# A two-part mLSTM and token-mixing kernel, rewritten: decays of chunk 0 from 0/1 products, values without padding, shared PSUM places, a new order of tasks

## Chip, core and metric

The kernel runs on one core of a Trainium2 chip. The metric is device time in microseconds (us) of that core for one launch; lower is better. PE is the engine for matrix products (PEld its weight loads), DVE the vector engine, ACT the scalar engine with its function tables, POOL the general engine, SP the engine that issues most DMA transfers.

## What is computed

Sizes: 4 batches, 8 heads, 768 tokens, 40 values per head; 320 channels. The first part is an mLSTM: per head a state `C` (40x40) and a vector `n` decay and grow from token to token, and are read with the query.

```python
m_new = np.maximum(f_gate[:, :, t] + m, i_gate[:, :, t])
f_stab = np.exp(f_gate[:, :, t] + m - m_new)
i_stab = np.exp(i_gate[:, :, t] - m_new)
C = f_stab[..., None, None] * C + i_stab[..., None, None] * np.einsum('bhd,bhe->bhde', vt, kt)
n = f_stab[:, :, None] * n + i_stab[:, :, None] * kt
h_tilde = np.einsum('bhde,bhe->bhd', C, qt)
denom = np.maximum(np.abs(np.einsum('bhd,bhd->bh', n, qt)[:, :, None]), 1.0)
y[:, :, t] = 1.0 / (1.0 + np.exp(-o_gate[:, :, t])) * h_tilde / denom
```

The second part takes these rows `x` (4 x 768 x 320), turns each number by an angle, mixes tokens, and ends with a channel product:

```python
theta = x @ w_theta
zr, zi = x * np.cos(theta), x * np.sin(theta)
u = x + np.einsum('ts,bsd->btd', w_tok_r, zr) + np.einsum('ts,bsd->btd', w_tok_i, zi)
return u + np.maximum(u @ w_ch, 0.0)
```

## The kernel before

The 768 tokens are cut into six chunks of 128. A **unit** is one batch in one chunk (24 units, four to a chunk), a **pair** is two batches in one chunk (12 pairs). Within a chunk the mLSTM is done as masked attention; what earlier chunks leave comes in through the state.

**Gates** (`gate_part`, `gates_rest`): scans on DVE give each head's running sums of decays; they are written to DRAM (`g_first`, `g_rest`, `e_d`) and read back by `unit_loads` as tables that are the same on all partitions (`dt`, `eb`). Only unit 0 gets its table from PE (`spread`, L741).

**A unit** (`score`, `attention`): PE forms scores `sc` (L337), upper and lower 64 rows in turn, two heads at a time. ACT takes exponentials of `dt` with a bias per head (L360), POOL masks them (L364), DVE multiplies with the scores (L370). PE multiplies these weights with the values into `ph` (L382), and q, faded on DVE or POOL (L455), with the state (L377). The values are stored with zeros between the heads, so that a product of each head writes 123 columns, the 41 of three heads. DVE or ACT, DVE, DVE form size, maximum and reciprocal of the denominator (L391, L389, L395, L396); the output gate is scaled on POOL, DVE or ACT (L404, L402) and applied on DVE (L411). Keys are faded (L417, L419), PE forms the chunk's new state `st` (L425), DVE or ACT masks it into `cn` (L436, L440), and POOL or DVE adds it to the faded state (L448, L449, or L445).

**A pair** (`mixer`, `mix_part`, `mix`): PE turns the rows over (L560) and forms angles with a three-product split of numbers into high and low parts (L597, 18 products of 320 columns; channel block 2 in 64-row halves). Angles are rounded (L605, L607, L610), sine and cosine taken on ACT, multiplied with x and split again (L633, L636, L639). Then ten groups of six products of 384 columns mix tokens (L506), each group into one of two single PSUM banks (`ps_m`, tile `pm`); DVE adds each into `acc` (L513; chunk 0 L515 to L520). Weights arrive as 64-bit numbers and are split on DVE, ACT and POOL (`split`, L249 to L271).

**The end** (`channel`, L864 to L894): `acc` is split once more into `u`, and 204 products (48 over 64 rows) form the channel product with ReLU and sum on DVE.

**What sets the order**: a table of numbers, `ORDER`, names every task with its engine letter (V DVE, A ACT, G POOL, T PE, D SP), and `Plan.issue` writes them out in that order; each engine takes its instructions strictly in it. PSUM has eight banks: `sc0`, `sc1`, `ph`, `st`, the pair `pt`, and two of `pm`.

Of the kernel before, what the change touches and what calls it, by code (L numbers as in the profile page):

```python
# [21 lines left out]
HP = 9  # L22
NR = B * HP
E1 = D + 1
VG = 7 * E1
NG = 3 * B
QR = 64 + D
NT = B * DM // P
TH = S // 2
GROUPS = tuple((c,) for c in range(NC))  # L30
# [4 lines left out]
PIECE = 512  # L35


PAR = dict(load=-8328, wload=-8347, sgload=-2808, exps=860, score=867, mult=173, pv=-1216, X=-126, st=1806, upd=-1500,
           tr=-2000, theta=-645, ang=-1907, z=-255, mix=3437, wdec=2329, sig=-5151, grest=-643, wch=22567, u0=32000,
           u1=32000, out0=18267, out1=27456, tab=3960, slack=155, zm0='V', zm1='V', zl0='G', zl1='G', wlo='G', cup='G',  # L40
           ulo='GG', ab='A', s0=-2609, s1=-11037, s2=-11454, s3=-9068, wth=-6011, w0=-734, w1=-3805, w2=-1051,
           wdup=-8318, kh='A', qh='A', kl='G', ql='V', qk=-6000, m0=7, m1=23, gst=2, slackT=67, dsg0=19, dsg1=140,
           did=61, dh0=123, dt0=115, dth=133, dh1=81, dd1=70, dt1=150, dw=145, du2=89, dmask=26, dgr=25, sg0=-1128,
           cw=17892, clr=-6830)
# [8 lines left out]
99V 52D 45A 183V 102V 109T 103V 100A 184V 262A 189V 185G 268D 186V 253G 110A 263T 46V 269D 111V 104G 53A 190T 112A
249D 54V 113A 280A 193V 101G 267D 55V 114V 271V 319D 115A 56V 254A 116V 191V 117G 192V 57G 322D 194T 48V 118A 272A
255G 256V 327A 49V 257T 195V 273G 230D 196V 119V 236D 50A 328G 270T 264A 258V 259V 260V 320A 339D 274V 51G 340D 261V
265G 133T 231A 123T 237A 323D 134A 197V 281T 232V 198A 143T 324D 233V 325T 238V 242D 275T 124A 144A 329V 199G 345A
410D 202V 343T 341D 276V 335G 128T 277V 326V 140T 203V 282A 428D 204V 129A 141V 278G 200A 411D 125T 142A 279V 283G
234A 330T 126V 127A 201V 342D 239V 416A 336T 235G 429D 331V 220T 337V 346G 223T 412D 221V 222V 243A 338G 347V 213T
240A 224A 135T 392D 434A 214V 417G 130T 136V 413D 332V 244V 414T 132A 137A 284T 131V 333G 418V 483D 120T 285A 344G
334V 138T 121V 435G 286V 122A 205T 139A 245V 287V 415G 210T 246A 398D 207V 241G 206V 288T 211V 212V 247V 393A 424G  # L60
228T 289V 353G 208T 290V 229A 399V 291A 354T 400V 292A 348T 394V 395V 432T 209A 349V 404D 350V 396A 293V 215T 296V
294A 225T 501D 216V 351G 297A 436V 217A 397G 481D 227A 218T 352V 226V 295V 405A 419T 219V 298G 430D 355V 401V 303T
420V 356G 484D 482A 357T 304V 487T 502D 358V 425T 421V 359V 402A 422G 313T 426A 431D 360V 403G 309T 423V 489A 485D
314V 427V 361T 310V 406V 486D 433G 311T 554D 362V 507A 490G 301T 363V 572D 312V 497G 437T 491V 442A 508G 302V 488V
505T 364V 555A 573D 438V 439V 365A 407V 443T 509V 440G 299T 560D 444V 576T 445V 408A 590D 317T 441V 366G 578A 300V
498T 504D 318V 492T 369V 645D 409V 370V 371V 503D 561A 305T 367V 493A 494V 368V 307T 591D 306V 495G 499V 386T 506G
496V 308V 574D 446T 387V 500G 515A 382T 447V 378T 448V 596A 579G 575D 449V 516T 379V 450T 580V 586A 597G 383V 577V
594T 451V 376T 452V 663D 380T 598V 453A 454A 510T 377V 381V 562V 563V 388T 517A 592D 511V 455G 390T 564A 389V 372T
512V 456A 646D 565V 513A 391V 458G 649T 373V 374T 734D 457V 459A 384T 514V 518G 375V 643D 651A 581T 385V 556V 593D
# [12 lines left out]
779G 710T 835V 912D 836V 780A 841V 837G 963T 711V 782G 838V 704T 960D 698T 705V 783V 843T 781V 696T 699V 784G 846V
706T 965A 697V 842V 708T 707V 913D 725V 714T 726V 878D 727V 905T 715V 709V 966G 884D 844V 845V 787T 906A 962D 907V
908V 847T 909V 961D 788V 879V 967V 797T 974D 848A 885V 964V 793T 849V 798V 977T 794V 850V 801T 915V 851A 886V 919T
802V 887V 979A 852V 795T 976D 920V 855G 789T 796V 975D 921V 785T 922V 923V 790V 888A 924T 980G 786V 856A 968T 927V
889G 925V 857V 799T 853V 969A 970V 971V 700T 800V 854G 926V 791T 701V 978G 972V 864T 792V 880V 870T 865V 928T 871V
881V 882V 890D 981V 883G 874T 929V 1024D 862T 875V 930V 982T 863V 931A 891V 932A 892V 876T 983V 984V 893V 860T 985G
877V 1030D 894A 858T 986V 895G 861V 1022V 987T 859V 866T 990V 712T 988A 867V 989V 872T 933G 713V 991T 873V 936V 934V
937A 935G 803T 992V 868T 993V 938G 804V 869V 1023A 994A 945T 1025V 1026V 995A 951T 1027V 946V 1036D 1031A 996V 939T
1028A 952V 999G 997A 957T 940V 1029V 949T 1000A 958V 998G 1037A 943T 950V 1001V 947T 944V 1032V 1046A 1014T 1033V  # L90
1034V 1015V 1035G 948V 1038V 1048A 1018T 1039V 1020T 1019V 1040A 1049V 1012T 1021V 1041V 1087A 1002T 1013V 1042G 955T
1003V 941T 956V 1047V 1052A 1004T 942V 1043G 1044A 1010T 1005V 1006T 1011V 1079V 1083A 953T 1045G 1007V 1008T 954V
1050V 1016T 1009V 1051G 1081A 1059T 1017V 1085A 1054T 1084G 1060V 1056T 1055V 1053G 1061T 1057V 1058D 1086V 1066T
1062V 1082G 1063D 1080G 1074T 1067V 1064T 1075V 1088G 1089T 1065V 1068D 1099T 1090V 1111T 1100V 1094T 1112V 1076T
1095V 1071T 1077V 1078D 1069T 1072V 1101T 1070V 1073D 1109T 1102V 1103D 1106T 1110V 1113D 1096T 1107V 1091T 1097V
1098D 1104T 1092V 1093D 1105V 1108D
""".split()


class Plan:  # L100


    def __init__(self):
        self.waiting = []

    def add(self, eng, us, prio, fn, after=(), table=None, cols=0, follow=(), bank=None, pick=None, dmas=1):
        alts = None
        if isinstance(eng, dict):
            alts, fn0 = eng, fn
            eng = pick or next(iter(alts))  # L110
            us = alts[eng]
            fn = lambda: fn0(t.eng)
# [5 lines left out]
    def clash(self, some, others):  # L118

        for a in some:  # L120
            for b in others:
                a.clash.append(b)
                b.clash.append(a)
# [14 lines left out]
def mlstm_mixer(ctx: ExitStack, tc: tile.TileContext, gates, qk, q3, tok, og,  # L138
# [662 lines left out]
    for n in range(NU):  # L801
# [9 lines left out]
        if n % 2:  # L811
            mixer(q)
# [168 lines left out]
```

## Time and profile before

| | |
|---|---|
| three timed runs | 396.33, 392.63, 395.36 us, median 395.36 |
| profiled execution | span 388.3 us; the page gives no time of its own beside it |
| busy in that span | PE 329.2 (85%), PEld 297.2, DVE 300.0 (77%), ACT 205.2 (53%), POOL 164.2 (42%) |
| DMA | 66.81 MB in 51,506 packets |
| chain that ended last | PE 34%, DVE 28%, DMA 23%, ACT 6%, issue 5% |
| first and last token-mixing product | 72.2 us, 344.2 us |

A row of the page's groups gives line, engine, operation, output<-input, shape and count, then busy us, the mean ns of one, and the idle time before it with what ended it. In the slices each digit is a fortieth of the span, in tenths of busy time.

### The profile page before, as it was taken

How to read it: one execution, taken by the hardware profiler on the slowest of the kernel's cores; microseconds unless marked ns; L12 is line 12 of the kernel's file. 1: busy time of each engine (PE TensorE's matmuls, PEld its weight loads, DVE VectorE, ACT ScalarE, POOL GpSimd, SP SyncE). 2: the span in 40 equal slices, each digit the busy share in tenths (PEclk: the TensorE clock that was granted, in tenths of full speed). 3: DMA queues.
4: the chain of work that ended last, by engine and by line, in shares of the span. 5: the costliest groups of instructions: out<-in, count | busy, mean ns of one | idle time of the engine just before them, and what ended most of it. 6: DMA issues, size and time to landing. Idle time of an engine off the chain costs nothing.

```text
span 388.3 us, 6289 instructions
## 1 busy us (share of the span) xinstructions
PE 329.2 (85%) x2231; PEld 297.2 (77%) x2231; DVE 300.0 (77%) x559; ACT 205.2 (53%) x478; POOL 164.2 (42%) x146
## 2 busy tenths in 40 slices
PE   4468743986899979889899889999989987999995
PEld 3357632885798869779789789989988976888884
DVE  4858728995688878698699989999999989854222
ACT  2675748982653964788788755843440433320000
POOL 1518233564627245265113755555133442475000
PEclk9657966999899999999999999999999999999999
DMA  6979999699517999559783794838640101302134
GB/s 169 259 275 321 251 261 265 164 265 218 163 57 219 252 232 241 134 152 292 192 263 93 237 290 147 215 92 229 190 158 13 56 1 41 69 0 83 41 122 162
DMA packets 51506, 66.81 MB, mean 172 GB/s; under 512 B 3112, under 2 KB 39436, under 8 KB 51476
## 3 DMA queue, kind: packets, MB, share of 16 engines
q1 hardware_dynamic: 50259, 65.12, 59.1%
q0 software_dynamic: 1216, 1.31, 1.8%
q8 instruction: 17, 0.28, 0.3%
q14 instruction: 14, 0.11, 0.1%
HBM read 60.97 MB, written 4.13 MB: 168 GB/s over the span
## 4 chain that ended last, share of the span: by engine, by line
PE 34%; DVE 28%; DMA 23%; ACT 6%; issue 5%; SPq 2%; POOL 1%; DVEq 0%; POOLq 0%; ACTq 0%
PE pm L506 12%; PE pm L888 10%; DMA eb<-e_d 8%; DMA q_t<-in_q 5%; DVE acc L513 5%; PE pt L597 3%; PE ph L382 3%; DMA dt<-g_rest 3%; DMA sg<-in_og 3%; ACT dt L360 2%; DVE val L257 2%; PE sc L337 2%; DVE dt L370 2%; DVE val L261 2%; DVE C L445 2%
## 5 line engine op out<-in xcount | busy, mean ns | idle before, releaser
L506 PE MATMUL pm<-w,z 128*128 128x384 f32 x480 | 96.7, 349 | 9.2 <-ACT acc L515 5.3
L506 PEld LDWEIGHTS pm<-w,z 128*128 128x128 f32 x480 | 83.4, 191 | 14.1 <-ACT acc L515 5.9
L382 PE MATMUL ph<-tok_t,dt 128*128 128x123 f32 x384 | 57.1, 287 | 5.8 <-DMA tok_t<-in_tok 4.8
L360 ACT ACTIVATE dt<-dt,bwT 128x128 f32<-128x128 f32 x184 | 56.1, 390 | 11.1 <-DMA dt<-g_rest 8.1
L513 DVE TENSOR_TENSOR acc<-pm,acc 128x384 f32<-128x384 f32 x100 | 53.6, 549 | 8.5 <-PE pm L506 8.0
L382 PEld LDWEIGHTS ph<-tok_t,dt 128*128 128x128 f32 x384 | 51.0, 201 | 7.1 <-ACT acc L582 2.9
L506 PE MATMUL pm<-wsm,z 128*128 128x384 f32 x240 | 46.6, 344 | 7.4 <-DVE acc L513 7.3
L506 PEld LDWEIGHTS pm<-wsm,z 128*128 128x128 f32 x240 | 41.0, 188 | 11.2 <-DVE acc L513 11.1
L364 POOL TENSOR_SCALAR_AFFINE_SELECT dt<-dt 128x1024 f32<-128x1024 f32 (+1 forms) x26 | 30.2, 1162 | 38.8 <-ACT dt L360 35.7
L888 PE MATMUL pm<-u,w 128*128 128x384 f32 (+1 forms) x204 | 40.2, 351 | 0.0
L597 PE MATMUL pt<-wthp,xs 128*128 128x320 f32 (+1 forms) x198 | 32.3, 339 | 7.5 <-DVE xs L576 7.5
L888 PEld LDWEIGHTS pm<-u,w 128*128 128x128 f32 (+1 forms) x204 | 33.0, 187 | 7.0 <-issue 7.0
L597 PEld LDWEIGHTS pt<-wthp,xs 128*128 128x128 f32 (+1 forms) x198 | 26.0, 196 | 12.5 <-issue 12.4
L404 POOL TENSOR_TENSOR sg<-sg,den 128x320 f32<-128x320 f32 x15 | 13.0, 867 | 46.9 <-DVE den L396 46.5
L337 PE MATMUL sc<-qk 40*128 40x128 f32 x368 | 27.6, 291 | 5.1 <-DMA qk<-in_qk 5.1
L894 DVE SCALAR_TENSOR_TENSOR acc<-pm,acc 128x384 f32<-128x384 f32 x20 | 11.1, 557 | 26.7 <-PE pm L888 26.7
L370 DVE TENSOR_TENSOR dt<-sc,dt 128x512 f32<-128x512 f32 x46 | 29.4, 678 | 2.4 <-POOL dt L364 2.4
L337 PEld LDWEIGHTS sc<-qk 40*128 40x128 f32 x368 | 23.2, 193 | 9.8 <-issue 4.5
L377 PE MATMUL ph<-C,q_t 120*128 120x123 f32 x120 | 23.7, 279 | 3.9 <-DVE X L411 2.7
L377 PEld LDWEIGHTS ph<-C,q_t 120*128 120x128 f32 x120 | 18.8, 190 | 5.3 <-issue 1.9
L417 ACT ACTIVATE tok_t<-tok_t,bwT 128x40 f32<-128x40 f32 x64 | 14.7, 314 | 10.5 <-DMA tok_t<-in_tok 10.5
L455 POOL TENSOR_TENSOR q_t<-q_t,eb 120x384 f32<-120x384 f32 x11 | 12.4, 1127 | 18.2 <-DMA eb<-e_d 18.2
(117 smaller groups left out, 552.9 us busy)
## 6 DMA issues: line engine op xcount, KB each, us to landing
tok_t<-in_tok SPq DMA_DIRECT2D x24, 610.5 KB
dt<-g_rest SPq DMA_DIRECT2D x20, 512.0 KB
qk<-in_qk SPq DMA_DIRECT2D x24, 416.0 KB
raw<-in_wtok SPq DMA_DIRECT2D x18, 512.0 KB
sg<-in_og SPq DMA_DIRECT2D x12, 320.0 KB
out<-acc SPq DMA_DIRECT2D x10, 384.0 KB
q_t<-in_q SPq DMA_DIRECT2D x20, 180.0 KB
eb<-e_d SPq DMA_DIRECT2D x60, 60.0 KB
```

The source lines that it names most:

```text
L337: nc.tensor.matmul(u.sc[s][:, hp], u.qk[rows, 1, hp], u.qk[rows, 0, hp], start=True, stop=True)
L360: nc.scalar.activation(u.dt[:, h, :], src, AF.Exp, bias=bwT[:, c, r:r + 1])
L364: nc.gpsimd.affine_select(d, d, pattern=[[0, h1 - h0], [1, P]], compare_op=ALU.is_ge, fill=0.0, base=0, channel_multiplier=-1)
L370: nc.vector.tensor_mul(d2[:, s], u.sc[s], d2[:, s])
L377: nc.tensor.matmul(u.ph[:, gg * 3 * E1:(gg + 1) * 3 * E1], u.q3[:, gg, :], C[b][:, gg, :], start=True, stop=False)
L382: nc.tensor.matmul(u.ph[:, gg * 3 * E1:(gg + 1) * 3 * E1], u.dt[:, h, :], among(h), start=(c == 0 and h == 3 * gg), stop=(h == min(3 * gg ...
L404: ENG[e].tensor_mul(u.s3, u.s3, u.den.broadcast_to([P, H, D]))
L417: nc.scalar.mul(k3[:, h], k3[:, h], bwT[:, c, 64 + HP * b + h:64 + HP * b + h + 1])
L506: nc.tensor.matmul(pm[:, :TH], x.z[:, a, s, j * P:(j + 1) * P], w[x.c][:, b, s, th * TH:(th + 1) * TH], start=(k == 0), stop=(k == last))
L513: nc.vector.tensor_add(a, pm[:, :TH], a)
L597: nc.tensor.matmul(S_.th[:, b - b0, :DM], p.xs[a0:a1, a, k, :], wt5[a0:a1, s, k, :], start=(n == 0), stop=(n == 8))
L888: nc.tensor.matmul(pm[:, :TH], E_.w[s][a0:a1, col:col + P], us[pr, k][a0:a1, a, ts], start=(n == 0), stop=(n == 3 * len(ks) - 1))
```

## The change

The whole body is rewritten. What is computed and the split into chunks, units, pairs and groups stay. By parts:

- **Chunk 0's decays**: the running sums of all heads are split into high and low parts on two halves of the partitions, and four products per unit of a 0/1 matrix with them (L278, L283) write all eight heads' exponents into two PSUM banks. ACT takes two exponentials of 512 columns per unit there (L401) in place of eight of 128 with a bias. The DRAM tables serve chunks 1 to 5 only.
- **DRAM layout**: decay tables are stored chunk by chunk, so that a unit's table is one run of 4 KB per partition (L405), q and its decays one of 1.5 KB (L393, L394; the decays in one transfer in place of three). Tokens take 688 numbers in place of 1221.
- **Values without zeros**: a head's product writes its own 41 columns (L446).
- **Output**: the maximum with 1 is taken in the gate's instruction, on DVE always (L457).
- **State**: faded in place (L488, L490) and grown straight from PSUM in three instructions per unit (L501).
- **Halves**: the 64-row products of angles and of the channel part stand in pairs, lower and upper in turn (L537, L655).
- **PSUM**: three places of two banks (`two`) for scores, chunk 0's decays, transposes, angles, mixing groups and the channel part, and two single banks (`one`) for `ph` and `st`. A mixing group is now 12 products into a two-bank place, gathered in one instruction of 768 columns (L590).
- **Weights**: split in pieces of 768 columns; copies between partition halves on ACT and DVE, where POOL issued DMAs.
- **Order**: a new table of 1009 entries.

```diff
+    two = slots("two", 3, [2, 512], pool=ps)
+    one = slots("one", 2, [512], pool=ps)
...
+    def assemble(u):
+        lw = hi_t.t.rearrange("p a s n -> p (a s n)")[:, P:2 * P]
+        gm = GMt[u.c]()
...
+        for f in range(2):
+            r = slice(64 * f, 64 * f + 64)
+            nc.tensor.matmul(u.dd.t[:, f, :], selr[r, 33 + b:34 + b].broadcast_to([64, P]), gm[r], start=False, stop=True)
...
-            src = g_d[0][rows, :] if c == 0 else g_d[1][rows, (c - 1) * P:c * P]
-            nc.sync.dma_start(u.dt, src.unsqueeze(0).broadcast_to([P, H, P]))
+            load(f"dt{n}", lambda: dma(u.E.t.rearrange("p h t -> p (h t)"), g_d[c, b * H:(b + 1) * H].rearrange(
+                "h t -> (h t)").unsqueeze(0).broadcast_to([P, H * P])), [u.E], n - 2.2)
...
-                        nc.tensor.matmul(u.ph[:, gg * 3 * E1:(gg + 1) * 3 * E1], u.dt[:, h, :], among(h),
+                    nc.tensor.matmul(u.ph.t[:, h * E1:(h + 1) * E1], u.E.t[:, RANK[h], :], v1,
...
+            nc.vector.scalar_tensor_tensor(s3(), u.den.t.broadcast_to([P, H, D]), 1.0, s3(), op0=ALU.min, op1=ALU.mult)
...
+                    nc.vector.scalar_tensor_tensor(cv[:, :k, j], st[:, :k, j], own[:KD, j:j + 1], cv[:, :k, j],
+                                                   op0=ALU.mult, op1=ALU.add)
...
+        def rest(e):
+            for l, (x, y) in enumerate(parts):
+                for b in range(2):
+                    rows = slice(64 * b, 64 * b + 64)
+                    nc.tensor.matmul(th.t[:, b, :DM], xs.t[rows, x, 2], wt5[rows, y, 2], start=False, stop=(l == 2))
...
+                for t in range(2):
+                    k = 0
+                    for s in (1, 0):
+                        for x, y in parts:
+                            nc.tensor.matmul(pm.t[:, t, :TH], z.t[:, x, s, j * P:(j + 1) * P], wv(c, y, s, t),
+                                             start=(k == 0), stop=(k == 5))
+                            k += 1
...
+                add(f"ga{q}{j}", "V", lambda e, j=j, pm=pm, av=av: nc.vector.tensor_add(av, pm.t[:, :, :TH], av), [pm],
```

Three places in the order show what moves. First SP, after its first two transfers. Before (`dt` is a decay table, `tok_t` tokens, `wsm` the gates):

```order
L296 DMA qk<-in_qk 104x1024
L173 DMA g_first<-wsm 36x128
L296 DMA qk<-in_qk 104x1024
L701 DMA sg<-in_og 128x640
L302 DMA dt<-g_first 128x1024
L306 DMA tok_t<-in_tok 128x1221
L173 DMA g_rest<-wsm 36x640
```

Of the change:

```order
L343 DMA raw_80<-in_wth 128x480
L389 DMA qk_96<-in_qk 128x1024
L389 DMA qk_97<-in_qk 128x1024
L343 DMA raw_81<-in_wth 128x480
L379 DMA sg_106<-in_og 128x640
L390 DMA tok_99<-in_tok 128x688
L379 DMA sg_107<-in_og 128x1280
```

No decay table stands among the first transfers any more; the angle weights have moved to the front, and tokens are shorter.

Second PE, where a pair's angles are formed in the middle of the kernel. Before (`pm` a mixing group, `pt` angles, `ph` output):

```order
L425 MATMUL st<-tok_t 120x123 x3
L506 MATMUL pm<-w,z 128x384 x12
L597 MATMUL pt<-wthp,xs 128x320 x18
L506 MATMUL pm<-w,z 128x384 x12
L377 MATMUL ph<-C_97,q_t 128x123
L382 MATMUL ph<-tok_t,dt 128x123 x3
```

Of the change:

```order
L446 MATMUL one_76<-tok_101,E_93 128x41 x2
L531 MATMUL two_73<-wth,xs_89 128x320 x12
L537 MATMUL two_73<-wth,xs_89 128x320 x6
L425 MATMUL two_72<-qk_98 128x128 x8
L425 MATMUL two_74<-qk_97 128x128 x8
L480 MATMUL one_76<-tok_101 120x123 x2
L480 MATMUL one_76<-tok_101 120x82
L575 MATMUL two_73<-w_899,z_77 128x384 x12
L575 MATMUL two_74<-w_899,z_77 128x384 x12
```

Angles, two units' scores and two mixing groups follow one another through the same three places, 72 to 74; the 64-row products (L537) stand by themselves.

Third DVE, around a unit's output. Before:

```order
L391 TENSOR_SCALAR den<-ph 128x8
L395 TENSOR_SCALAR den<-den 128x8
L396 RECIPROCAL den<-den 128x8
L404 TENSOR_TENSOR sg<-sg,den 128x320
L411 TENSOR_TENSOR X<-ph,sg 128x320
L436 TENSOR_TENSOR cn<-st,mask 120x369
L445 SCALAR_TENSOR_TENSOR C_97<-C_97,eb,cn 120x123 x3
L513 TENSOR_TENSOR acc<-pm,acc 128x384
```

Of the change:

```order
L451 TENSOR_SCALAR den_109<-one_75 128x8
L452 RECIPROCAL den_109<-den_109 128x8
L457 SCALAR_TENSOR_TENSOR sg_107<-den_109,sg_107 128x320
L519 TENSOR_TENSOR xs_89<-two_73,xs_89 128x640
L488 TENSOR_SCALAR C_113<-C_113,eb_104 120x123 x3
L463 TENSOR_TENSOR X_85<-one_75,sg_107 128x320
L590 TENSOR_TENSOR acc<-two_72,acc 128x768
L590 TENSOR_TENSOR acc<-two_74,acc 128x768
```

One instruction of the denominator is gone, the state is faded here ahead of its growth, and a gather covers two banks.

More of the change, by code (lines that the diff above doesn't have):

```diff
@@ L1 @@
 import math
-from types import SimpleNamespace
 from contextlib import ExitStack
@@ L34 @@
 WCOLS = 1792
[L35 to L44, printed above, removed]
@@ L53 @@
[L53 to L57, printed above, removed]
@@ L100, with __init__ @@
+class Task:
+    def __init__(self, name, engs, fn, uses, after, step, table, half, swap):
+        self.name, self.engs, self.fn, self.uses, self.after = name, engs, fn, uses, after
+        self.step, self.table, self.half, self.swap, self.eng = step, table, half, swap, engs[0]
 class Plan:
     def __init__(self):
[L104 to L112, printed above, removed]
[L113 to L116 removed]
@@ L118, in clash, with add, run @@
[L118 to L123, printed above, removed]
+        self.tasks = []
+    def add(self, name, engs, fn, uses=(), step=0.0, after=(), table=None, half=False, swap=None):
+        t = Task(name, engs, fn, tuple(uses), tuple(a for a in after if a is not None), step, table, half, swap)
+        for u in t.uses:
+            u.uses += 1
+        self.tasks.append(t)
+        return t
+    def run(self, t, eng):
+        for u in t.uses:
+            if u.at is None:
+                u.take()
+        t.eng = eng
+        t.fn(eng)
+        for u in t.uses:
+            u.uses -= 1
+            if u.uses == 0:
+                u.kind.free.append(u.at)
@@ L238, in mlstm_mixer, with slots @@
-    halves = []
-    def split(hi, lo, raw, n, prio, loaded, after=(), scale=None):
+    def slots(name, k, shape, dtype=F32, pool=pool):
+        tiles = [pool.tile([P, *shape], dtype, name=f"{name}{i}") for i in range(k)]
+        return Slots(name, [lambda d, t=t: t for t in tiles])
+    TCOL = P + 3 + 33 + 4 + 4 + 1
+    tab = pool.tile([P, TCOL], F32, name="tab")
+    ident, own, chosen, mask4, minus = (tab[:, a:b] for a, b in (
+        (0, P), (P, P + 3), (P + 3, P + 40), (P + 40, P + 44), (P + 44, P + 45)))
@@ new lines, in mlstm_mixer, with load @@
+    qk_k = slots("qk", 3, [2, 4 * P], pool=ap)
+    tok_k = slots("tok", 3, [TOK], pool=ap)
+    q3_k = slots("q3", 2, [3, P], pool=ap)
+    eb_k = slots("eb", 2, [3, P], pool=ap)
+    sg_k = slots("sg", 2, [B * DM], pool=ap)
+    den_k = slots("den", 3, [H, 1], pool=ap)
+    C = [ap.tile([KD, 9, E1], F32, name=f"C{b}") for b in range(B)]
+    def load(name, fn, uses=(), step=0.0, after=()):
+        return add(name, "D", lambda e: fn(), uses, step, after)
+    dma = nc.sync.dma_start
+    gt = Tile(w_k)
@@ L263, in split @@
-        t = first = add({"A": us - 0.08, "V": us}, None, prio, size, [loaded, *after, *(x[1] for x in halves[-2:-1])],
-                        follow=[x[0] for x in halves[-1:]])
-        t = add("V", us * 2.2 + 0.23, prio, upper, [t])
-        low = t = add("V", us, prio, lower, [t])
-        one = {"A": us - 0.08, "V": 0.07 + n * 0.00052}
-        if scale is not None:
-            t = add(one, None, prio, lambda e: SCALE[e](T.v, T.v, scale), [t])
-        t = add(one, None, prio, lambda e: COPY[e](hi(), T.v), [t])
@@ L785, in mlstm_mixer @@
-    first = [(PAR["wth"] + k, turn_part, (k,)) for k in range(2)]
-    p = -1e9
-    for k in range(3):
-        p = max(p, PAR[f"w{k}"])
-        first.append((p, mix_weights, (0, k)))
-    for _, part, a in sorted(first, key=lambda x: x[0]):
-        part(*a)
-    wth_ready = [ends, [add("G", 2.1, PAR["wdup"], lambda k=k: copies(k, k - 3, k - 2), ends) for k in (3, 4)]]
-    turned, stored = {0: turned0}, {}
-    def gates_rest(after):
-        stored[1], done, stored[2] = gate_part(1, NC, 2000 + PAR["grest"], l_gr, after)
-        for k in range(1, NC):
-            turned[k] = done
-        return [done]
@@ L906, in mlstm_mixer @@
+    gates_rest()
+    for n in range(NU):
+        if n % B == 0 and n > 0:
+            mix_weights(n // B)
+            gate_out(n // B, n - 1.0)
+        attention(n)
+        if n % 2:
+            mixer(n // 2)
+    names = {f"X{n}" for n in range(NU - 4, NU)} | {f"ph{n}" for n in range(NU - 4, NU)} | {f"up{NU - 5}", f"wane{NU - 5}"}
+    channel()
     plan.issue()
```

1215 lines of the change are left out of this document (524 added, 691 removed).

## Prediction

> **What bounds the kernel now.** I read the page's slices first, then the busy times in three stretches, cut at the first token-mixing product (72 us) and at the last (344 us).
>
> ```profile
> PE   4468743986899979889899889999989987999995
> DVE  4858728995688878698699989999999989854222
> PEclk9657966999899999999999999999999999999999
> DMA  6979999699517999559783794838640101302134
> ```
>
> ```profile
> core 0: us, PE busy (x) PEld busy (x) DVE busy (x) ACT busy (x) POOL busy (x), PEclk, DMA share, GB/s
> 0.00:72.00 72.00, 42.11 (x279) 36.82 (x281) 48.95 (x98) 45.35 (x117) 28.45 (x34) 0.76 0.88 250
> 72.00:344.00 272.00, 246.83 (x1752) 227.53 (x1749) 237.19 (x440) 158.43 (x361) 125.32 (x108) 0.99 0.61 165
> 344.00:389.00 45.00, 40.23 (x205) 32.88 (x204) 13.90 (x22) 1.41 (x2) 10.44 (x6) 1.00 0.22 88
> ```
>
> There are three limits, one after the other. In the start the DMA engines are busy 88% and PE only 58%. In the middle PE (91%) and DVE (87%) are both nearly full, and the chain of waits goes back and forth between them. In the end only PE works:
>
> ```profile
> 245.25 4.25 PE pm L506 x24
> 250.13 2.60 PE pt L597 x18
> 344.16 40.08 PE pm L888 x204
> 384.27 0.56 DVE acc L894
> ```
>
> So the sum has three terms, 72 + 272 + 44.3 = 388.3 us of span. The timed runs (392.6 to 396.3, median 395.4) lie 4 to 8 us above the span of this one profiled execution; I add 7.1 us to mine. ACT and POOL are busy under 60% in the middle and set no term.
>
> **The start.** It is held by transfers of small pieces.
>
> ```profile
> DMA packets 51506, 66.81 MB, mean 172 GB/s; under 512 B 3112, under 2 KB 39436, under 8 KB 51476
> q1 hardware_dynamic: 50259, 65.12, 59.1%
> dt<-g_rest SPq DMA_DIRECT2D x20, 512.0 KB
> eb<-e_d SPq DMA_DIRECT2D x60, 60.0 KB
> tok_t<-in_tok SPq DMA_DIRECT2D x24, 610.5 KB
> ```
>
> The 39,436 packets under 2 KB are the decay tables, q and its decays, read in rows of 128 numbers. In the change these stand one behind the other in DRAM, so the same bytes go in rows of 1.5 or 4 KB. The three tables of chunk 0 are no longer loaded (1.5 MB); PE assembles them with 16 products of 512 columns in place of 8 of 128. The values without zeros make tok 344 KB in place of 610. The three transfers of eb become one, so SP issues 40 fewer. By the order, some 18 MB are issued up to the first mixing product, as many as now (250 GB/s by 72 us), but three more units of attention are done by then. Price of small rows: in the end stretch, where only large rows run, the engines move 88 GB/s at a share of 0.22, 400 GB/s when full; over the start it is 250 at 0.88, 284 when full. So 18 MB take 45 to 64 us of full engines.
>
> DVE then has 56 us of work before its first gather (49 now, plus the three units). At today's 68% in the start that is 82 us, at the 87% of the middle it is 64. With the transfers eased I take **70 us**, between 60 and 82.
>
> **The middle, PE.** These rows give the pace of products.
>
> ```profile
> 113.30 0.80 PE L425 MATMUL st<-tok_t 128*120 128x123 f32 x6
> 113.94 0.39 PE L377 MATMUL ph<-C,q_t 120*128 120x123 f32 x2
> 114.16 0.83 PE L382 MATMUL ph<-tok_t,dt 128*128 128x123 f32 x6
> 114.83 0.39 PE L377 MATMUL ph<-C,q_t 120*128 120x123 f32 x2
> 116.48 1.16 PE L337 MATMUL sc<-qk 40*128 40x128 f32 x16
> 117.58 2.37 PE L506 MATMUL pm<-w,z 128*128 128x384 f32 x12
> ```
>
> ```profile
> L425 PEld LDWEIGHTS st<-tok_t x78: 179/183/185, 113.1 to 249.8; 128*120 128x120 f32 x78
> L382 PEld LDWEIGHTS ph<-tok_t,dt x272: 190/192/192, 114.1 to 304.6; 128*128 128x128 f32 x136
> ```
>
> The 192 products of weights and values (two records each) now have 41 columns in place of 123. That looks like two thirds saved, but the pace is not set by the columns alone: both kinds above stream 123 columns, and the one with 120 stationary columns comes every 107 ns (113.30 to 113.94, six), the one with 128 every 112 (114.16 to 114.83). Their weight loads differ too, 183 against 192 ns. The stationary side stays 128x128, so I take **no saving** here. The other bound is the fastest record in the trace, the 69 ns of the scores (116.48 to 117.58, sixteen): 17 units are left behind the first mix, times 16 records, times 43 ns, 12 us.
>
> The Trainium skill, TensorE: Matmul & The Clock Gate, section LDWEIGHTS, says that a weight load takes its columns divided by 1.2 in ns, whatever the rows. By it 128 columns cannot come faster than 107 ns and the saving would be 1.4 us; the 107 and 112 ns above lean that way.
>
> The products over 64 rows now stand in pairs, lower and upper half in turn. The scores are written so, and a record takes 69 ns where one of nearly as many columns over all rows takes 112. In the angles (18 products in 2.60 us, 144 ns each, the halves no faster now) six of 18 pair up: three times 144 ns, 0.43 us for each of ten pairs left, 4.3 us. Two units' values (2 x 2.54), two scores (2 x 1.10) and one state (0.64) go ahead of the first mix, 7.9 us. So PE has 246.8 - 12.2 = 234.6 us, 0.95 of now.
>
> **The middle, DVE.**
>
> ```profile
> L513 DVE TENSOR_TENSOR acc<-pm,acc 128x384 f32<-128x384 f32 x100 | 53.6, 549 | 8.5 <-PE pm L506 8.0
> L584 DVE TENSOR_TENSOR acc<-pt,acc 128x640 f32<-128x640 f32 x10 | 8.2, 817 | 0.2
> L395 DVE TENSOR_SCALAR den<-den 128x8 f32<-128x8 f32 x24 | 6.9, 287 | 1.4 <-ACT den L389 1.1
> L607 DVE TENSOR_SCALAR rr<-pt 128x640 f32<-128x640 f32 x8 | 6.6, 819 | 2.3 <-PE pt L597 2.2
> L639 DVE TENSOR_TENSOR z<-rr,z 128x640 fp32r<-128x640 f32 x7 | 6.4, 912 | 0.1
> L445 DVE SCALAR_TENSOR_TENSOR C<-C,eb,cn 120x123 f32<-120x123 f32 x18 | 7.5, 469 | 1.0 <-ACT cn L440 0.9
> L436 DVE TENSOR_TENSOR cn<-st,mask 120x369 f32<-120x369 f32 x9 | 4.8, 530 | 0.8 <-POOL dt L364 0.5 <-PE st L425 0.3
> L436 DVE TENSOR_TENSOR C<-st,mask 120x369 f32<-120x369 f32 x4 | 2.1, 524 | 0.0
> L419 DVE TENSOR_TENSOR tok_t<-tok_t,bwT 128x360 f32<-128x360 f32 x2 | 1.4, 682 | 0.0
> L517 DVE TENSOR_TENSOR acc<-pm,acc 128x128 f32<-128x128 f32 x10 | 2.7, 278 | 7.3 <-PE pm L506 7.3
> L404 DVE TENSOR_TENSOR sg<-sg,den x6: 491/890/1637, 43.1 to 292.1; 128x320 f32<-128x320 f32 x6
> L867 DVE TENSOR_TENSOR u<-acc,u 128x768 fp32r<-128x768 f32 x3 | 4.3, 1418 | 0.0
> ```
>
> Less: 50 gathers of 768 columns for 100 of 384. From 549 ns at 384 and 817 at 640 a column costs 1.05 ns, so 768 take 951: 54.9 to 47.6, -7.3. The maximum of the denominator goes into the gate, -6.9. Rounding goes to ACT in 7 of 8 cases, -5.7; fewer splits of z, sizes and copies fall to DVE, about -10. Wider weight splits, -2, fewer products of q, -2. More: the gate is always on DVE, 24 at 0.49 to 0.89 us in place of six, taken at 0.75, +12.3. The state: 48 additions straight from PSUM at some 0.28 us and 27 decays in place at about 0.2, 18.8 us for 14.4 now (4.8 + 2.1 + 7.5), estimated from L517 and L395, +4.4. Fades, 18 thirds of L419's 682 ns, and seven more sizes, +4.4; splits of u, +6.6; copies across halves that were POOL's DMAs, +1.6. Sum about -5. The three units done ahead take 7 more out: 237.2 - 12 = 225 us, also 0.95.
>
> Both full engines lose 5%, and I let the middle keep its shares: 272 x 0.95 = **258 us**, from 247 (PE at 95%) to 276.
>
> **The end.** 48 of the 204 products pair up, 24 x 196 ns = 4.7 us off 40.1; the last ReLU has 768 columns, +0.4. **40 us**, 36 to 45.
>
> Sum: 70 + 258 + 40 + 7 = **375 us**, 5% less. A measurement of this kernel tells about 1% from no change.
>
> **Rivals.** (a) *Quick and dense:* the start ends when DVE's 56 us do, at 60, and the middle runs with PE at 95%: 60 + 247 + 40 + 7 = 354 us. For it: one gather and one wait in place of two. Against: DVE must then hold 91%.
>
> (b) *DVE pays for POOL:* the gate's rows above run from 491 to 1637 ns for one shape; in-place decays, fades and gates read SBUF alone, as it does. If they cost 16 us more than taken, DVE has 241 us, at 87% 276: 70 + 276 + 40 + 7 = 393 us. The Trainium skill, SBUF — State Buffer, section SBUF: two separate sides, says that a DVE instruction with two SBUF inputs and a POOL instruction exclude each other for the whole of whichever came first; the spread of L404 agrees.
>
> (c) *Halves don't pair:* the rows of two halves go to two banks, and their pace may stay: 375 + 4.3 + 4.7 = 384 us.
>
> (d) *Slower, from the shared PSUM places:* scores, transposes, angles and mixing all take one of three two-bank places, where mixing had two banks of its own, scores two, and the rest a pair.
>
> ```profile
> PEld pm L506 <- DVE acc L513: 15.4, 21, 2.3
> PE pm L506 <- DVE acc L513: 9.6, 13, 2.0
> ```
>
> Today 21 groups wait 0.73 us each for a gather. PE takes its work in order, so a mixing group without a place stops the scores behind it, which feed the next weighing. Decisive from 20/60 = 0.33 us for each of 60 groups; at 0.6 us (a gather of 951 ns in place of 549 before the place is free) it gives 375 + 36 = 411 us.
>
> **Chances.** Forecast 0.46, (a) 0.22, (b) 0.14, (c) 0.07, (d) 0.11. The range goes from just under (a) to just over (b), 350 to 397. Faster by over 1%: forecast, (a), (c) and a small part of (b), 0.80; within 1%: most of (b), 0.09; slower 0.11.
>
> **What will show it.** First mixing product at 60 to 82 us with DMA under 80% busy before it; records of weights and values still about 107 ns apart; angles in about 2.2 us for 18 products; gathers near 951 ns; DVE busy near 295 us; under 37 us from the last mix to the last product. Wrong if PE's waits for gathers exceed 20 us, or if the first mix comes no earlier than 82 us.

## The result and the profile after

The changed kernel takes 367.99 us (median of 4, 365.28 to 372.19) where the kernel before takes 394.74: ratio 0.9327, interval 0.9235 to 0.942. In two further runs it took 364.98 (median of 6, 357.26 to 369.15) and 365.86 (0.9273, 0.9224 to 0.9322). In the profiled executions TensorE's clock opens, that is, goes from half to full, at different moments of the start, so I read two of them side by side: this one (372.19 us) and one of the next run (357.26 us). Slices of the first, then its three stretches, cut as in the prediction (same columns):

```profile
PE   1599998799969989989889899979889999799995
PEclk9755589589978989999999699999996999899999
```

```profile
0.00:71.40 71.40, 55.63 (x371) 52.33 (x371) 56.67 (x98) 45.10 (x93) 32.06 (x45) 0.72 0.75 258
71.40:333.10 261.70, 241.13 (x1671) 232.52 (x1672) 225.00 (x364) 137.87 (x261) 128.66 (x121) 0.94 0.43 143
333.10:371.00 37.90, 33.04 (x206) 30.70 (x204) 16.55 (x18) 0.84 (x1) 1.86 (x1) 0.98 0.27 105
```

The same for the execution of 357.26 us:

```profile
0.00:64.40 64.40, 51.60 (x370) 47.97 (x371) 52.60 (x90) 43.46 (x87) 31.23 (x42) 0.96 0.75 257
64.40:318.00 253.60, 235.76 (x1671) 227.25 (x1671) 224.57 (x373) 139.44 (x266) 130.79 (x124) 0.96 0.47 154
```

From the 3rd slice on PE is nearly always busy, where the prediction's slices have 3 to 8 before, though in the first execution its clock stands at 5, half, in the 3rd to 5th. The middle was 272 us and is 261.7 or 253.6, at about the same shares of PE and DVE and at a granted clock of 0.94 and 0.96 where it was 0.99; the end was 44.3 and is 37.4 to the end of the span (370.5), 37.5 in the second (355.5).

Groups of the second execution that answer to the prediction's rows (busy us, mean ns | idle before):

```profile
L446 PE MATMUL one<-tok,E 128*128 128x41 f32 x384 | 53.6, 286 | 1.2 <-DVE E L429 1.2
L590 DVE TENSOR_TENSOR acc<-two,acc 128x768 f32<-128x768 f32 x50 | 47.1, 949 | 12.7 <-PE two L575 12.4
L457 DVE SCALAR_TENSOR_TENSOR sg<-den,sg 128x320 f32<-128x320 f32 x24 | 15.2, 637 | 0.4
L501 DVE SCALAR_TENSOR_TENSOR C<-one,tab,C 120x123 f32<-120x123 f32 (+1 forms) x48 | 12.8, 319 | 0.0
L488 DVE TENSOR_SCALAR C<-C,eb 120x123 f32<-120x123 f32 x27 | 8.0, 351 | 0.0
L474 DVE TENSOR_TENSOR tok<-tok,fadeT 128x120 f32<-128x120 f32 x18 | 6.9, 435 | 0.0
```

The values of 41 columns (L446) cost nearly what those of 123 columns did (L382: 384 records, 57.1 us). And what mixing groups wait for a gather, in the first execution, by PE's weight loads and products:

```profile
PEld two L575 <- DVE acc L590: 3.8, 3, 2.6
```

```profile
PE two L575 <- DVE acc L590: 2.9, 2, 2.3
```

It was 15.4 and 9.6 us.

### The profile page after: what moved, and what is told of

Its sections match the earlier page's. It is cut to its first block, busy times and chain, and to the rows that moved or that the text cites. A ratio compares the mean times of both kernels' runs of the same rounds, so it can differ in the third digit from the quotient of the medians.

```text
span 370.5 us, 6031 instructions
## 1 busy us (share of the span) xinstructions
PE 329.8 (89%) x2244; PEld 315.6 (85%) x2244; DVE 298.2 (80%) x479; ACT 183.8 (50%) x353; POOL 162.6 (44%) x166
## 4 chain that ended last, share of the span: by engine, by line
PE 43%; DVE 32%; issue 9%; DMA 7%; ACT 5%; POOL 2%; SPq 0%; DVEq 0%; POOLq 0%; ACTq 0%
PE two L575 18%; PE two L645 8%; PE one L446 6%; DVE acc L590 4%; PE two L425 3%; DMA E<-g_d 3%; PE two L531 3%; DVE E L429 3%; DMA eb<-e_d 2%; DVE val L330 2%; DMA w<-in_gates 2%; PE one L480 2%; DVE C L501 2%; DVE val L327 2%; DVE val L323 1%
## 5 line engine op out<-in xcount | busy, mean ns | idle before, releaser
L575 PE MATMUL two<-w,z 128*128 128x384 f32 x720 | 142.5, 357 | 9.5 <-DVE E L429 3.3
L575 PEld LDWEIGHTS two<-w,z 128*128 128x128 f32 x720 | 134.1, 202 | 12.0 <-DVE E L429 3.8
L416 POOL TENSOR_SCALAR_AFFINE_SELECT E<-E 128x512 f32<-128x512 f32 x48 | 39.5, 835 | 58.1 <-ACT E L410 33.5
L590 DVE TENSOR_TENSOR acc<-two,acc 128x768 f32<-128x768 f32 x50 | 47.1, 949 | 15.9 <-PE two L575 15.7
L446 PE MATMUL one<-tok,E 128*128 128x41 f32 x384 | 58.1, 301 | 1.3 <-DVE E L429 1.3
L446 PEld LDWEIGHTS one<-tok,E 128*128 128x128 f32 x384 | 56.7, 223 | 1.5 <-DVE E L429 1.5
L410 ACT ACTIVATE E<-E,biasT 128x128 f32<-128x128 f32 x160 | 49.7, 392 | 11.4 <-PE one L446 7.8
L425 PE MATMUL two<-qk 40*128 40x128 f32 x384 | 29.7, 309 | 5.7 <-ACT E L401 3.4
L429 DVE TENSOR_TENSOR E<-two,E 128x1024 f32<-128x1024 f32 (+1 forms) x28 | 29.4, 1060 | 4.4 <-DMA E<-g_d 1.5
L645 PE MATMUL two<-u,w 128*128 128x384 f32 x156 | 28.3, 338 | 0.0
```

The lines of the kernel that those rows point to most:

```text
L410: nc.scalar.activation(u.E.t[:, r], u.E.t[:, r], AF.Exp, bias=biasT[:, c, b * H + r:b * H + r + 1])
L416: nc.gpsimd.affine_select(d, d, pattern=[[0, 4], [1, P]], compare_op=ALU.is_ge, fill=0.0, base=0, channel_multiplier=-1)
L425: nc.tensor.matmul(u.sc.t[:, f, hp], u.qk.t[rows, 1, hp], u.qk.t[rows, 0, hp], start=True, stop=True)
L429: add(f"wg{n}{a}", "V", lambda e, a=a, z=z: nc.vector.tensor_mul(u.E.t.rearrange("p (f k) t -> p f (k t)", f=2)[:, a:z], u.sc.t[:, a:z], u ...
L446: nc.tensor.matmul(u.ph.t[:, h * E1:(h + 1) * E1], u.E.t[:, RANK[h], :], v1, start=(c == 0), stop=(c == 0 or h == hs[-1]))
L575: nc.tensor.matmul(pm.t[:, t, :TH], z.t[:, x, s, j * P:(j + 1) * P], wv(c, y, s, t), start=(k == 0), stop=(k == 5))
```

## Experiments

The lines named are those of the changed kernel. Spans are cut at the first and last mixing product, as above.

**Does the weight load or the number of columns set the pace of the values?** First the kernel once more, and two edits of the values. In the first edit three heads' values stand where one head's and zeros belong; in the second, five of eight heads leave out half of the tokens in chunks 1 to 5.

> The changed kernel once more, for a profile at the full clock and as the mark for the others. By the prediction's stages: first mixing product at about 70 us, last one before 330 us, end some 37 us later; ratio to the kernel before 0.92 to 0.945. If the lower clock of the first profile hid a gain, the middle stage is 5 us or more shorter here.

```diff
-v1 = u.tok.t[:, 9 * D + h * E1:9 * D + (h + 1) * E1]
-nc.tensor.matmul(u.ph.t[:, h * E1:(h + 1) * E1], u.E.t[:, RANK[h], :], v1,
...
+n1 = len(hs) * E1
+v1 = u.tok.t[:, 9 * D + 3 * g * E1:9 * D + 3 * g * E1 + n1]
+nc.tensor.matmul(u.ph.t[:, 3 * g * E1:3 * g * E1 + n1], u.E.t[:, RANK[h], :], v1,
...
```

> Each of the 192 products of weights and values streams 123 (or 82) columns again in place of 41, with nothing else changed: loads, loads' bytes and stationary sides stay (each head's weights meet all three heads' values, so the output is not the reference's). Theory A, the weight load of 128 columns sets the pace: a record stays at 107 to 115 ns in the middle, the time rises by 0 to 3 us. Theory B, the columns set the pace: a record goes from below 112 to about 112 ns, PE's busy time there rises by 10 us or more, the time by 5 to 12 us.

```diff
-nc.tensor.matmul(u.ph.t[:, h * E1:(h + 1) * E1], u.E.t[:, RANK[h], :], v1,
+k = P if c == 0 or h == hs[-1] else 64
+nc.tensor.matmul(u.ph.t[:k, h * E1:(h + 1) * E1], u.E.t[:, RANK[h], :k], v1,
```

> Five of eight heads' products in chunks 1 to 5 load 64 stationary columns in place of 128 (half of the tokens of these heads are left out, so the output is not the reference's); moving columns stay 41. Theory A, the load sets the pace: these 200 records come every 55 to 65 ns, PE has 8 to 10 us less work, the time falls by 3 to 8 us as PE is one of two full engines. Theory B, the moving columns or the issue of an instruction set the pace: records stay above 95 ns and the time within 2 us.

Measured: again 364.98; the wide form 354.48 (ratio 0.9001, 0.8946 to 0.9057); the half load 367.65 (0.9336, 0.9284 to 0.9388). In again the middle is 8 us shorter than in the first execution, at a clock of 0.96 for 0.94. Not only is nothing saved by 41 columns, by the medians the 123 columns are faster by 10 us, which neither theory had. One unit's products in the middle, from the timelines of again, the wide form and the half load (start, duration, records):

```profile
161.13 0.45 PE L442 MATMUL one<-C,q 120*128 120x123 f32 x2
161.42 0.77 PE L446 MATMUL one<-tok,E 128*128 128x41 f32 x6
162.01 0.46 PE L442 MATMUL one<-C,q 120*128 120x123 f32 x2
...
163.58 0.63 PE L516 MATMUL two<-tab,X 128*128 128x128 f32 x4
```

```profile
160.03 0.44 PE L442 MATMUL one<-C,q 120*128 120x123 f32 x2
160.31 0.83 PE L447 MATMUL one<-tok,E 128*128 128x123 f32 x6
160.97 0.39 PE L442 MATMUL one<-C,q 120*128 120x123 f32 x2
...
162.50 0.71 PE L517 MATMUL two<-tab,X 128*128 128x128 f32 x5
```

```profile
164.98 0.77 PE L447 MATMUL one<-tok,E 128*64 128x41 f32 x6
165.58 0.46 PE L442 MATMUL one<-C,q 120*128 120x123 f32 x2
165.98 0.77 PE L447 MATMUL one<-tok,E 128*64 128x41 f32 x6
```

Six records take 0.59 us with 41 columns and 0.66 with 123; the two products of the state beside them take 0.29 and 0.28. The unit as a whole takes 2.45 us (161.13 to 163.58) or 2.47 (160.03 to 162.50). So at full clock the columns are worth 0.02 us a unit.

In the half load the six records take 0.60 us, but only four of them have half the load. The weight loads by themselves show more; four in the half load, then four in again:

```profile
164.98 0.31 PEld L447 LDWEIGHTS one<-tok,E 128*64 128x64 f32 x4
163.10 0.53 PEld L446 LDWEIGHTS one<-tok,E 128*128 128x128 f32 x4
```

One of these loads lasts 0.14 us and 0.19, so they begin (0.31 - 0.14) / 3 = 57 ns apart with 64 columns and (0.53 - 0.19) / 3 = 113 with 128, and the products follow at that pace (medians of 59 and 111 ns in the middle). Half the load is twice as quick: the load sets the pace of 41 columns, and 123 columns come no slower (every 112 ns). What is gained is lost where the load changes: the first full load comes 186 ns behind the last half one, and the two products of the state take 0.40 us in place of 0.29. So the pace is theory A's and the time theory B's.

The 10 us of the wide form must lie elsewhere. In its start the clock opens earlier. The chain of waits there, in again, in the first execution and in the wide form:

```profile
26.40 6.76 PE one L446 x32
33.16 3.71 PE two L425 x32
39.38 3.57 PE one L446 x32
```

```profile
39.40 6.68 PE one L446 x32
```

```profile
26.36 4.34 PE one L447 x32
30.70 1.99 PE two L425 x32
36.43 9.28 DMA qk<-in_qk
```

Chunk 0's values come every 211 ns (6.76 / 32) at first and every 112 ns (3.57 / 32) later, the scores every 116 ns (3.71 / 32), and every 62 in the wide form. The clock says the same for the first execution, in stretches of its start:

```profile
26.00:33.00 7.00, 7.00 (x35) 7.00 (x33) 4.70 (x11) 4.32 (x8) 1.30 (x2) 0.50 0.67 200
39.00:46.00 7.00, 7.00 (x35) 7.00 (x33) 3.86 (x8) 6.06 (x14) 1.49 (x2) 0.50 0.33 108
```

PE is busy without a gap and at half clock from 26 to 46 us. In the wide form the full clock is there some 2 us after the values begin (4.34 us are 8 records at 211 ns and 24 at 110); then the transfer of qk takes PE's place in the chain. In again it comes at 39 us, in the first execution past 46; there the second 32 values cost 3.1 us more, and the first mix comes at 71.4 us instead of 64.4.

The traces of all runs of this document agree. By their record of the clock, with 41 columns it opens at 39.0 to 40.5 us in three executions (again, and below the letters and two gathers) and at 48.4 to 58.6 in the other seven; with 123 columns (the wide form, and two runs below) at 27.8 to 30.3. The first mix comes at 64.4 to 65.3 us in the three, at 65.8 to 71.4 in the seven, and at 64.4 to 65.1 with 123 columns. So a late clock costs up to 7 us of the start, but one that opens before 39 us brings nothing more: in all three with 123 columns the transfer of qk, which lands at 45.2 to 45.7 us, then stands in the chain to the first mix. Against again's profiled execution (357.26 us) the wide form's (354.63) gains less than 3 us. The 10 us are those to the median; that the unprofiled executions of 363 us and more opened late too is likely and not shown.

**The zeros put back,** so that each head meets its own values only.

```diff
-v1 = u.tok.t[:, 9 * D + h * E1:9 * D + (h + 1) * E1]
-nc.tensor.matmul(u.ph.t[:, h * E1:(h + 1) * E1], u.E.t[:, RANK[h], :], v1,
...
+n1 = len(hs) * E1
+at = 9 * D + (7 * g + 2 * (h - hs[0])) * E1
+nc.tensor.matmul(u.ph.t[:, 3 * g * E1:3 * g * E1 + n1], u.E.t[:, RANK[h], :], u.tok.t[:, at:at + n1],
...
```

The values lie as v 0 0 v 0 0 v, so that three heads' columns begin at each, two of them zero.

> Edit: the values get their zeros back: for each head the moving operand of L446 holds the three heads of its group with zeros in the two others' places (123 and 82 columns, one accumulation group per three heads, as in the kernel before), everything else as in the changed kernel; the token tile and its load grow by 41 x 10 numbers a partition (24 loads of 4.4 KB a partition instead of 2.8 KB, 5 MB more in all). Theory B (the columns are free because a record of these products takes 99 to 110 ns either way, and the 41-column stream is even the slower form): 350 to 359 us, near the 354.5 us of the run with wide products, the added 5 MB hidden in a middle where the DMA share is 0.45. Theory A (the gain of the run with wide products came from something else, such as its fewer distinct values or a lucky set of executions, or the load is not hidden): 365 us or more, as the changed kernel again (365.0 us).

Measured: 357.73 (0.9068, 0.8974 to 0.9162), theory B. First mix at 65.1 us; the middle (253.8) is that of again. The 5 MB more are hidden. Its first 16 values take 3.43 us, 214 ns each, and the next 16 take 2.03, 127 each: the clock opens some 4 us after they begin. In the middle it stands at 0.99, and PE is busy 231.4 us for 235.8, which does not shorten it. Its profiled execution (358.14 us) is as long as again's (357.26); the 7 us are again those to the median.

**Does the order of the halves matter?** The 64-row products of angles and channel, three lower then three upper ones, instead of in turn:

```diff
-for l, (x, y) in enumerate(prods):
-    for jj in (j0, j0 + 3):
+for jj in (j0, j0 + 3):
+    for l, (x, y) in enumerate(prods):
```

> Products over 64 rows stand three lower then three upper again, in the angles and in the channel part. Theory A, halves written in turn run side by side: angles go back from about 2.2 to 2.6 us for 18 products, the channel part's 48 from about 5 to 9.4 us; the end stage grows by 4 to 5 us, the time by 6 to 9 us. Theory B, adjacent halves in any order overlap, or the gain is elsewhere: time within 2 us.

Measured: 360.46 (0.9124, 0.9059 to 0.9188). Timelines of again and of this kernel, angles first, then the first 64-row products of the end:

```profile
241.99 2.00 PE L531 MATMUL two<-wth,xs 128*128 128x320 f32 x12
243.92 0.71 PE L537 MATMUL two<-wth,xs 64*128 64x320 f32 x6
244.47 0.72 PE L425 MATMUL two<-qk 40*128 40x128 f32 x10
...
322.45 1.32 PE L655 MATMUL two<-u,w 64*128 64x384 f32 x12
```

```profile
250.33 2.00 PE L531 MATMUL two<-wth,xs 128*128 128x320 f32 x12
252.26 0.71 PE L537 MATMUL two<-wth,xs 64*128 64x320 f32 x6
252.81 0.39 PE L425 MATMUL two<-qk 40*128 40x128 f32 x4
...
328.77 1.33 PE L655 MATMUL two<-u,w 64*128 64x384 f32 x12
```

Both orders are the same to 0.01 us, and in both the halves run side by side. The first two records of the angles' halves, in again and in this kernel:

```profile
243.92 0.42 PE L537 MATMUL two<-wth,xs 64*128 64x320 f32 x2
252.26 0.42 PE L537 MATMUL two<-wth,xs 64*128 64x320 f32 x2
```

Two records together take 0.42 us where one lasts 0.41: a lower and an upper half begin 3 ns apart in again and 10 in this kernel. That is the first form of theory B; turns are not needed. In the angles it is not new either: in the kernel before, with three lower and then three upper ones, 33 of 36 such pairs began within 20 ns of one another. In the end it is: 6 of 24 pairs before, all 24 now, since there the halves stood in threes, mostly of one kind, between products over 128 rows. And TensorE goes from 128 rows to 64 and back 4 times, where it did so 14 times. From record to record, products of one kind begin 173 ns apart, a pair of halves as well; each way to 64 rows and back adds 0.40 us. So 18 new pairs x 173 ns = 3.1 us and 10 x 0.40 = 4.0 us make 7.1 of the 7.2 us that the end gained. Two rows of the second execution's page show it; before they were 31.1 and 11.1 us (L888, one line for both shapes):

```profile
L645 PE MATMUL two<-u,w 128*128 128x384 f32 x156 | 28.3, 338 | 0.0
L655 PE MATMUL two<-u,w 64*128 64x384 f32 x48 | 5.3, 351 | 0.0
```

**Do the small pieces of the transfers hold the start?** Rows of 512 bytes again for the decays, the queries and the state's factors:

```diff
-g_d = dram.tile([NC, R, P], F32, name="g_d")
-e_d = dram.tile([NC, R + 1, P], F32, name="e_d")
+g_d = dram.tile([NC, R, 2 * P], F32, name="g_d")[:, :, :P]
+e_d = dram.tile([NC, R + 1, 2 * P], F32, name="e_d")[:, :, :P]
```

> Edit: the rows in DRAM of the decays, the state's factors and the queries are 1024 bytes apart with 512 bytes used, so that their loads (L393, L394, L405) go in pieces of 512 bytes as in the kernel before; the same bytes, some 30,000 packets more; the compute is the same. Theory D (the start became shorter because the loads go in larger pieces: 39,436 packets under 2 KB became 7,700): the first mixing product comes 4 us or more later than in the changed kernel (64.4 us), at 68 to 74 us, and the time rises by 3 to 10 us. Theory O (the start became shorter by the order of its tasks and by the assembled decays of chunk 0, the size of the pieces does not matter): first mixing product at 63 to 66 us, time unchanged within 3 us.

Measured: 366.79 (0.9394, 0.9328 to 0.946), first mix at 70.4 us. By the letter that is theory D's 68 to 74, but the run does not decide: the clock opens late here (49.7 us), the second 32 values take 6.68 us, and from 26 to 70 us the chain that ended last has no transfer in it. With large rows the first mix came at 71.4 us in the first execution, where the clock opened at 48.8, and at 70.8 in the run again2 below, where it opened at 58.6. So the 27,500 packets more show no cost in this start; in all the run is some 5 us slower than again2 (0.9394 against 0.9273), and the trace does not show where. Small rows with an early clock were not tried. With the zeros, where the clock opens early, DMA is busy 85% of the start and 15 us of the chain to the first mix are transfers (qk and E, behind 38 us), so small rows may cost there. For the changed kernel my account of the start falls.

**Which engine sets the middle?** Work left out, of DVE (the sign step of the mixing weights) and of PE (the last small product of 96 of the 120 mixing sums):

```diff
-nc.vector.scalar_tensor_tensor(vi(), words(1), -0x40000000, vi(), op0=ALU.bitwise_and, op1=ALU.bitwise_or)
+pass
```

> Edit: the DVE instruction that puts the sign into the rounded mixing weights (L327, one of the rounding chain) is left out everywhere, so the mixing weights are not the reference's; DVE has some 16.6 us less to do, PE exactly the same. Theory P (PE sets the end of the middle: busy 231 of 249 us there): the time falls by less than 4 us, 361 to 366 us. Theory V (DVE's work, which PE waits for in turns, sets it, as the quarter of the chain on DVE says): the time falls by 8 us or more, 350 to 357 us.

```diff
+last = 4 if t or j < 3 else 5
+if k > last:
+    break
...
-start=(k == 0), stop=(k == 5))
+start=(k == 0), stop=(k == last))
```

> Edit: 96 of the 720 mixing products (L575) are left out, the last of the six or of the five per output for 32 of 40 pieces and so on, so the mixed values are not the reference's; PE has some 17 us less to do, DVE exactly the same. Theory P (PE sets the end of the middle): the time falls by 12 us or more, to 344 to 353 us. Theory V (DVE sets it): the time falls by less than 5 us, 360 to 366 us.

Measured: 358.31 (0.9119, 0.9012 to 0.9226) and 357.95 (0.9159, 0.9087 to 0.9232). Both lie between the two theories' figures. The middles, first without DVE's, then without PE's work:

```profile
68.60:313.90 245.30, 230.13 (x1672) 221.67 (x1672) 217.53 (x361) 140.26 (x269) 127.08 (x123) 0.99 0.48 158
```

```profile
70.60:321.30 250.70, 223.07 (x1576) 211.34 (x1576) 226.50 (x372) 139.96 (x269) 127.97 (x123) 0.96 0.48 155
```

Beside 253.6 to 261.7 us, 7 us less on DVE bring 8 us or more, and PE's own busy time falls by 6 (230.1 for 235.8) with the same products, at a clock of 0.99 for 0.96. 12.7 us less on PE bring 3 us or more; its idle time in the middle rises from 18 to 28 us. DVE weighs more, but neither stands alone. Each is one profile, on a chip on which the changed kernel was not run.

**Lighter DVE, and one more edit against the gathers,** beside the changed kernel on the same chip. The letters move 18 tasks of DVE's to ACT and six fades to POOL (19 and five, says the expectation); a further kernel has letters and zeros:

```diff
-100V 166V 300V 320V 600V 683V   40V 177V 202V 363V 513V 656V 715V 802V 806V 809V 813V   258V 269V 408V 708V 713V 719V 789V   3A
+100G 166G 300G 320G 600G 683G   40A 177A 202A 363A 513A 656A 715A 802A 806A 809A 813A   258A 269A 408A 708A 713A 719A 789A   3V
...
-nc.vector.tensor_add(av, pm.t[:, :, :TH], av)
+for t in range(2):
+    nc.vector.tensor_add(av[:, t], pm.t[:, t, :TH], av[:, t])
```

> The changed kernel unchanged, on the chip of the three runs beside it, so that they have a base of their own. Both theories: 357 to 369 us, as in its ten executions so far, first mixing product between 64 and 72 us, 253 to 262 us from the first to the last mixing product.

> Edit: letters of the order alone: 19 tasks of DVE's go to ACT (the absolute values and upper halves of the mixing weights, some upper halves of x and z, 0.55 to 1.0 us each), 5 fades go from DVE to POOL (three instructions of 0.44 to 0.54 us each), one small task comes to DVE; the place of each in the order is kept. DVE has some 18 us less to do (294 to about 276), ACT some 14 more (184 to 198), POOL some 9 more (164 to 173), PE the same. Theory V (DVE's turn in the chain sets the middle, as the two runs with work left out gave it: 8.4 us less from the first to the last mixing product for 11 us less on DVE, 2.9 us less for 17 us less on PE): 5 to 12 us less than the changed kernel beside it, the middle at 240 to 249 us. Theory P (PE sets the middle and the two runs only fell differently): within 3 us of it.

> Edit: the values with their zeros again (moving operand of 123 or 82 columns) and the same letters as in the run beside it. Theory V and columns free: the sum of both, 345 to 353 us, the fastest. Theory P: PE's busy time was the same in the run with the zeros, so 355 to 361 us as that run alone.

> Edit: each of the 50 gathers that reads two PSUM banks in one instruction of 768 columns (L590, 949 ns) becomes two of 384 columns, as in the kernel before, where the pair took 2 x 549 = 1098 ns: 7.4 us more on DVE, nothing else. Theory V: 4 to 9 us more than the changed kernel beside it, mostly between the first and the last mixing product. Theory P: within 2 us of it.

Measured: 365.86 for again2; 352.72 with the letters (0.8975, 0.8936 to 0.9014); 350.07 with letters and zeros (0.8908, 0.886 to 0.8957), the fastest; 363.77 with two gathers (0.9201, 0.9138 to 0.9265). Middles of again2 and of the letters:

```profile
70.80:327.10 256.30, 236.68 (x1671) 227.74 (x1671) 228.82 (x372) 140.13 (x269) 128.36 (x123) 0.96 0.46 153
```

```profile
64.50:313.30 248.80, 235.41 (x1671) 226.26 (x1672) 211.19 (x343) 150.96 (x283) 138.47 (x136) 0.96 0.48 157
```

17.6 us less on DVE shorten the middle by 7.5 us (by 4.8 against again's 253.6): theory V, though less than one for one; PE now works 95% of it. The other 6.3 us of span are the start (64.5 for 70.8), where the second 32 values take 3.59 us: the clock opened early. All six executions of the letters lie between 352.3 and 354.9 us; whether the letters bring the early clock is not shown. Zeros and letters do not add up: their middle is 248.5 us, and the start had little left to give. The two gathers refute a figure of mine:

```profile
L592 DVE TENSOR_TENSOR acc<-two,acc 128x384 f32<-128x384 f32 x100 | 50.2, 546 | 10.6 <-PE two L575 10.6
```

100 of 546 ns would be 54.6 us; busy is 50.2, since two in a row overlap. One gather for two saves 3.1 us of DVE (50.2 to 47.1), and no time that could be measured; theory V's 4 to 9 us did not come.

## Why the prediction was right, and where not

- **The sum.** 375 was forecast, 365 to 368 measured; of three profiles the mean is 68.9 + 257.2 + 37.5 = 363.6 of span. The forecast had 70 + 258 + 40. The largest miss is the 7.1 us added for what lies around the span: an execution of the changed kernel takes 1.7 us more than its span (372.19 for 370.5). One of the kernel before takes 2.0 more (392.29 for 390.3), so its profiled span of 388.3 was that of a quick execution, and 5 of the 7.1 were its distance to the median, not to be added to the change.
- **Start.** 70 us was about right, for another reason than given. Not small pieces of transfers, which showed no cost in the start when put back, but PE sets it: in again the chain runs over PE without a break from 20.6 to 53 us, more than half of it at half clock. The step "it is held by transfers of small pieces" failed for the changed kernel; only with 123 columns, where the clock opened earliest, does a transfer hold it, at much the same 64 to 65 us. That the figure came out near is luck. How much the order and how much the assembled decays took off was not tried apart.
- **Middle.** PE was to be busy 234.6 us and is 235.8 to 241.1, DVE 225 and is 224.6 to 228.8; the shares stayed. PE's sum came out although the 4.3 us for the angles in it did not come. That both must shrink together was the right picture, as leaving out work on one alone shows.
- **Values: no saving.** Right, with its reason: the load sets the pace, 57 ns for 64 stationary columns and 113 for 128. It was too kind, for a cause that the forecast did not have: by the medians the 41 columns cost some 7 us (365 against 357.7 with zeros), and the traces show the clock opening later with them.
- **Halves in turn.** That halves pair was right, that turns are needed was not. The angles were misread: there the halves paired already, and the time from the first record to the next product is 2.48 us for 2.44, not 2.2. The end's "24 x 196 ns = 4.7 us" was mis-sized: 7.2 us were saved, 40.1 to 32.9 from last mix to last product, 3.1 of them by 18 new pairs and 4.0 by fewer changes between products over 128 and over 64 rows, which the forecast left out. The Trainium skill, TensorEngine Tiling (Array Packing), section Key Properties, says that changing the tiling mode drains TensorE. If a product over 64 rows is such a mode, the rows agree: the cost goes with the number of changes.
- **DVE.** 295 forecast, 293.7 to 298.2 measured. Gathers 949 ns (951), gate 0.61 to 0.73 us (0.75), growth 12.8 us for 48 (13.4), fades 0.44 to 0.54 us a third (0.23), the state's decay in place 0.32 to 0.40 (0.2). The errors cancel, which is luck. The gathers' -7.3 is -3.1 by the run with two gathers.
- **Rivals.** (d) is refuted: waits for gathers fell from 15.4 and 9.6 us to 3.8 and 2.9. (b) did not come: the gate has its low price. (c) is refuted, since halves pair; in the angles they did so before the change. (a) came in part: 357 us where the clock opened early.

Open: why the clock opens at 39 us in one execution and near 49 or 59 in another of the same kernel, and why narrow products open it later.

## What to carry to other kernels

Before narrowing a product, look whether its records get shorter, and at the granted clock around it: here the load set the pace, and with fewer columns TensorE stayed longer at half clock. Put products of one shape behind one another, lower and upper halves in one stretch; which half comes first does not matter. Where two engines are over 85% busy and wait for each other, move work from the one to engines at 50% before saving on either: 24 letters brought 13 us by the medians, nearly half of what the rewrite brought. In the profiles 5 to 7.5 us of it stand in the middle; the rest is the start, with its early clock.

## What the runs showed of the hardware

- In all ten executions with 41 columns TensorE kept half clock through the first 6.8 us of them (32 records, 211 ns each, without a gap), and in seven through the next 32 as well, all or in part; with 123 columns it had full clock 1.5 to 3.8 us after they began. The Trainium skill, TensorE: Matmul & The Clock Gate, section What's actually happening, gives some 3.4 us of sustained work for it. The wide products come near that; the narrow ones do not, nor do the 6 us of other products (scores, state, transposes) between the two stretches of values in the first execution.
- Two executions with the same 6.7 us for 32 values showed a clock of 0.50 (the first, above) and of 1.00 (again2) for that stretch, so the pace of the records tells more than the clock's column. The trace's record of the clock begins at 11.3 us in the first and at 58.6 in again2; the column stands at 1.00 where there is no record:

```profile
39.00:46.00 7.00, 7.00 (x35) 7.00 (x34) 3.95 (x9) 6.25 (x15) 1.50 (x2) 1.00 0.41 111
```

- Weight loads of 64 columns began 57 ns apart, of 128 columns 113 ns, and products of 41 columns followed at that pace; with 128 columns loaded, 123 columns came every 112 ns as well.
- Two products over 64 rows, one of the lower and one of the upper half, began 3 to 10 ns apart and took as long as one, in either order. A stretch of them between products over 128 rows cost 0.40 us more than its records.
